# A fused linear attention and gated MLP on one core: moving tiles 256 instead of 320 bytes behind the weights

## The chip, the cores and the metric

The kernel runs on one core of a Trainium2 chip. The metric is the device time of one execution in microseconds, as the median of several runs. Instructions run on TensorE (PE in the profile, with weight loads apart as PEld), VectorE (DVE), ScalarE (ACT), GpSimd (POOL) and the DMA queues that SyncE (SP) and GpSimd issue.

## The reference

All data are float32. The reference is, cut to what is computed:

```python
# q, k, v: (8, 8, 576, 64) = batch, heads, sequence, head size
q_s = softmax of q over the head size (1e-9 added to the sum)
k_s = softmax of k over the sequence  (1e-9 added to the sum)
kv  = einsum('bhsd,bhse->bhde', k_s, v)
att = einsum('bhsd,bhde->bhse', q_s, kv)
x   = att, heads side by side: 4608 tokens x 512
out = (sigmoid(x @ w_gate) * (x @ w_val)) @ w_out    # 512 -> 1536 -> 512
```

## The kernel before

The 4608 tokens are worked through in nine windows of 512. Window 0 runs in plain fp32 while the weights are still being loaded and prepared (`g1_0`, L617, for the first product of the MLP, `g2_0`, L644, for the second, `x_mm_0`, L566, for the attention). Its weights arrive as 64-bit words that VectorE and ScalarE put together into fp32. In windows 1 to 8 each fp32 number is split into a high and a low part of type fp32r, and each product is three matmuls: high by high, high by low, low by high.

A window w of 1 to 8 takes six steps, one for each pair of blocks of 128 hidden columns. In a step:

- `g1(w, p)` (matmuls at L662) computes gate and value with a Strassen-like scheme of seven block products `prod`, 12 matmuls each, 84 in all. Weights are `a_w` (three of the products) and `s_sb` (four), the moving operand is `c_hl`, 256 columns at a time.
- `h_split` splits the result into `h`, and `g2` of the step before (L730) computes 24 matmuls of 512 columns into four accumulators: weights `h`, moving operand `wo_hl`.
- beside it stand parts of the next window's attention: key softmax, the key-value product `k_mm` (L382, plain fp32, weights in `ring`), the query softmax and `x_mm` (L542, weights `kv_sb`, moving operand in `ring`). `x_mm` cuts a window's 512 columns in two where a batch of 576 tokens ends.

The order of the instructions is written out by hand (`tc.manual_schedule()`), engine by engine in the order of the code. `s_sb` is loaded again for each step by four transfers on GpSimd's queue (L282), `wo_hl` by two (L238).

The tiles lie in pools, one behind the other in each partition, in the order in which the pools are opened: const, bpad, bpool, cpool, apad, apool, two, wpad, wpool, four, ring, small. `bpad`, `apad` and `wpad` hold one unused tile each, whose width sets where the pools behind it begin. Weights lie in const (`s_sb`, `kv_sb`, `f_last`), apool (`a_w`, `f_w`) and two (`h`); moving operands in bpool and cpool (`c_hl`, `x_0`), wpool (`wo_hl`, `wo_t`) and ring. In a partition, 128 columns of weights are 512 bytes and 256 moving columns 1024, so the places in a tile at which the matmuls of L662 and L730 start lie alike modulo 512.

In the function below, what bears on the change are the pads and the matmuls named above.

Of the kernel before, what the change touches and what calls it, by code (L numbers as in the profile page):

```python
# [8 lines left out]
F32 = mybir.dt.float32  # L9
# [8 lines left out]
P = 128  # L18
# [34 lines left out]
def attn_moe(ctx: ExitStack, tc: tile.TileContext, qf, qn, qT, k, kT, v, wg, wv, wo, out):  # L53
# [5 lines left out]
    bpad = ctx.enter_context(tc.tile_pool(name="bpad", bufs=1))  # L59
    bpool = ctx.enter_context(tc.tile_pool(name="bpool", bufs=1))  # L60
    cpool = ctx.enter_context(tc.tile_pool(name="cpool", bufs=1))
    apad = ctx.enter_context(tc.tile_pool(name="apad", bufs=1))
    apool = ctx.enter_context(tc.tile_pool(name="apool", bufs=1))
    two = ctx.enter_context(tc.tile_pool(name="two", bufs=2))
    wpad = ctx.enter_context(tc.tile_pool(name="wpad", bufs=1))
# [1 line left out]
    four = ctx.enter_context(tc.tile_pool(name="four", bufs=4))  # L67
    ring = ctx.enter_context(tc.tile_pool(name="ring", bufs=11))
    small = ctx.enter_context(tc.tile_pool(name="small", bufs=2))
    bpad.tile([P, 128], F32, name="pad_b")  # L70
    apad.tile([P, 48], F32, name="pad_a")
    wpad.tile([P, 80], F32, name="pad_w")
    dpool = ctx.enter_context(tc.tile_pool(name="dpool", bufs=2, space=bass.MemoryType.DRAM))
    spool = ctx.enter_context(tc.tile_pool(name="spool", bufs=1, space=bass.MemoryType.DRAM))
    ps_acc = ctx.enter_context(tc.tile_pool(name="ps_acc", bufs=NT, space=bass.MemoryType.PSUM))
# [1050 lines left out]
```

## Time and profile before

| | |
|---|---|
| median of 3 runs | 974.13 us (973.41 to 974.25) |
| profiled execution | 974.62 us |
| its span, first to last instruction | 972.9 us |
| mean granted TensorE clock | 0.987 |
| TensorE busy | 948.6 us, 6062 matmul records |
| VectorE, ScalarE, GpSimd busy | 613.3, 488.6, 169.7 us |
| DMA | 257.79 MB, 265 GB/s on the mean |

The span is the time between the first and the last instruction; the execution's own time has what lies around it as well. A TensorE busy share counts overlapping matmuls once and says nothing on how densely they follow one another; for that the chain of work in order of time is read, where a run of matmuls of one line is one piece with its length and count. A plain fp32 matmul leaves two records, an fp32r matmul one.

### The profile page before, as it was taken

The numbers are of one execution on the slowest core, as the hardware profiler recorded it, in microseconds if no ns is written. First come the engines' busy times: TensorE is split into PE (matmuls) and PEld (weight loads), VectorE is DVE, ScalarE is ACT, GpSimd is POOL, SyncE is SP. The second block draws the span as 40 slices with busy tenths as digits, with TensorE's granted clock in tenths as the row PEclk, the third lists the DMA queues.
The fourth block names the chain that finished last, engine by engine and source line by source line (L and its number), as shares of the span: only waits on it lengthen the run. The fifth ranks groups of instructions, "written<-read, shape, count | busy, mean of one in ns | idle before, by whom it ended". The sixth has DMA issues, their size and how long they took to land.

```text
span 972.9 us, 15630 instructions
## 1 busy us (share of the span) xinstructions
PE 948.6 (98%) x6062; PEld 821.0 (84%) x6062; DVE 613.3 (63%) x1013; ACT 488.6 (50%) x824; POOL 169.7 (17%) x316
## 2 busy tenths in 40 slices
PE   5899999899999999999999999999999999999998
PEld 4544544699999999999999999999999999999997
DVE  7698878776567566755675667556754655564242
ACT  4589785563446354725372547354635333533222
POOL 0110001221122112211211212111212121212210
PEclk8899999899999999999999999999999999999999
DMA  9987485899699978999899979997998689858672
GB/s 320 353 243 264 181 292 169 304 357 326 203 246 360 300 249 202 381 288 280 187 378 301 270 166 381 318 271 157 381 302 258 203 249 311 240 173 257 200 209 70
DMA packets 93865, 257.79 MB, mean 265 GB/s; under 512 B 15264, under 2 KB 17568, under 8 KB 93024
## 3 DMA queue, kind: packets, MB, share of 16 engines
q0 software_dynamic: 43712, 168.32, 57.6%
q1 hardware_dynamic: 50080, 88.48, 31.5%
q8 instruction: 48, 0.79, 0.4%
q14 instruction: 25, 0.20, 0.1%
HBM read 228.20 MB, written 28.56 MB: 264 GB/s over the span
## 4 chain that ended last, share of the span: by engine, by line
PE 82%; DMA 6%; issue 5%; DVE 4%; ACT 2%; POOL 0%; SPq 0%; POOLq 0%; ACTq 0%; DVEq 0%
PE gv L662 48%; PE acc L730 27%; PE at L382 3%; PE gv L542 2%; DMA lent<-v_in 1%; DMA wo_raw<-wo_in 1%; PE acc L644 1%; DMA lent<-kT_in 1%; DMA ring<-qf_in 1%; DMA s<-s_sb 1%; PE at L542 1%; DMA lent<-k_in 1%; DVE s L250 1%; DVE s_sb L273 0%; DVE a_w L273 0%
## 5 line engine op out<-in xcount | busy, mean ns | idle before, releaser
L662 PE MATMUL gv<-c_hl,s_sb 128*128 128x256 f32 x2304 | 283.7, 278 | 0.0
L662 PEld LDWEIGHTS gv<-c_hl,s_sb 128*128 128x128 f32 x2304 | 275.0, 188 | 0.0
L730 PE MATMUL acc<-wo_hl,h 128*128 128x512 f32 x1152 | 272.3, 392 | 0.0
L730 PEld LDWEIGHTS acc<-wo_hl,h 128*128 128x128 f32 x1152 | 213.0, 188 | 44.5
L662 PE MATMUL gv<-c_hl,a_w 128*128 128x256 f32 x1728 | 225.5, 279 | 0.0
L662 PEld LDWEIGHTS gv<-c_hl,a_w 128*128 128x128 f32 x1728 | 214.5, 188 | 4.3 <-issue 1.0
L282 POOL DMA_DIRECT2D s_sb<-s x188 | 100.4, 534 | 312.5 <-PE gv L662 312.4
L688 DVE TENSOR_TENSOR sg<-gv,sg 128x512 f32<-128x512 f32 x48 | 33.2, 691 | 162.0 <-PE gv L662 161.8
L238 POOL DMA_DIRECT2D wo_hl<-wo x96 | 52.6, 549 | 296.0 <-PE acc L730 295.7
L680 ACT COPY sg<-gv 128x512 f32<-128x512 f32 x48 | 28.2, 588 | 120.4 <-PE gv L662 118.7
L690 ACT COPY sg<-gv 128x512 f32<-128x512 f32 x48 | 28.2, 587 | 105.9 <-PE gv L662 105.9
L617 PE MATMUL gv<-x,f_w 128*128 128x512 f32 x160 | 72.4, 606 | 3.5 <-ACT h L625 3.5
L692 DVE TENSOR_TENSOR sg<-sg 128x512 f32<-128x512 f32 x48 | 33.2, 692 | 60.0 <-ACT sg L690 60.0
L617 PEld LDWEIGHTS gv<-x,f_w 128*128 128x128 f32 x160 | 30.5, 194 | 41.7 <-issue 35.8
L713 DVE TENSOR_TENSOR h<-sg,h 128x1024 fp32r<-128x1024 f32 x48 | 58.8, 1226 | 1.6
L701 DVE TENSOR_TENSOR sg<-sg 128x512 f32<-128x512 f32 x48 | 33.3, 693 | 33.5 <-ACT sg L695 33.5
L695 ACT ACTIVATE sg<-sg 128x512 f32<-128x512 f32 x48 | 30.4, 633 | 47.7 <-DVE sg L694 47.7
L644 PE MATMUL acc<-wo_t,h 128*128 128x512 f32 x96 | 46.0, 625 | 5.6 <-DVE h L629 5.6
L685 ACT COPY sg<-gv 128x512 f32<-128x512 f32 x48 | 28.2, 587 | 38.8 <-PE gv L662 38.8
L682 ACT COPY sg<-gv 128x512 f32<-128x512 f32 x48 | 28.2, 587 | 38.4 <-PE gv L662 38.4
L644 PEld LDWEIGHTS acc<-wo_t,h 128*128 128x128 f32 x96 | 19.2, 202 | 30.1 <-issue 22.2
L694 DVE TENSOR_TENSOR sg<-gv,sg 128x512 f32<-128x512 f32 x48 | 33.2, 692 | 4.1
(152 smaller groups left out, 1040.5 us busy)
## 6 DMA issues: line engine op xcount, KB each, us to landing
s_sb<-s POOLq DMA_DIRECT2D x188, 512.0 KB, 7.4
wo_hl<-wo POOLq DMA_DIRECT2D x96, 512.0 KB, 6.3
s<-s_sb POOLq DMA_DIRECT2D x6, 2048.0 KB, 7.6
out<-x SPq DMA_DIRECT2D x36, 256.0 KB, 10.0
ring<-k_in SPq DMA_DIRECT2D x28, 256.0 KB, 13.8
ring<-qn_in SPq DMA_DIRECT2D x28, 256.0 KB, 9.9
q_b<-q_m_row SPq DMA_DIRECT2D x56, 128.0 KB, 8.9
ring<-qT_in SPq DMA_DIRECT2D x28, 256.0 KB, 8.7
```

The source lines that it names most:

```text
L238: nc.gpsimd.dma_start(out=t.rearrange("p h e -> p (h e)"), in_=wo_dram[2 * p + i].bitcast(F32R))
L282: nc.gpsimd.dma_start(out=s_sb[:, i].rearrange("p h n e -> p (h n e)"), in_=s_dram[p][:, i * n:(i + 1) * n].bitcast(F32R),)
L617: nc.tensor.matmul(ps[n], lhsT=w[:, kt // 2, sl], rhs=x_0[:, kt], start=(kt == 0), stop=(kt == NK - 1),)
L644: nc.tensor.matmul(acc[0][m], lhsT=h_0[j][:, m * P:(m + 1) * P], rhs=wo_t[j // 2][:, j % 2], start=(j == 0), stop=(j == NJ - 1),)
L662: nc.tensor.matmul(ps[:, n], lhsT=lh(kt), rhs=c_hl[i][:, x, kt], start=(first and n == 0 and kt == 0 and lh is wh and x == 0), stop=(last ...
L688: nc.vector.tensor_tensor(out=sg[:, 0], in0=rr, in1=sg[:, 0], op=ALU.add)
L692: nc.vector.tensor_tensor(out=sg[:, 3], in0=sg[:, 3], in1=sg[:, 2], op=ALU.add)
L694: nc.vector.tensor_tensor(out=sg[:, 1], in0=z, in1=sg[:, 1], op=ALU.add)
L695: nc.scalar.activation(sg[:, 0:2, 0], sg[:, 0:2, 0], AF.Sigmoid)
L701: tt(out=sg[:, 0:2, 0], in0=sg[:, 0:2, 0], in1=sg[:, 0:2, 1], op=ALU.mult)
L713: nc.vector.tensor_tensor(out=lo, in0=sg[:, :, 0], in1=hi.bitcast(F32), op=ALU.subtract)
L730: nc.tensor.matmul(acc[w][m], lhsT=h[lh][:, i, sl], rhs=o[i][:, rh], start=(at == 0 and i == 0 and lh == 0 and rh == 0), stop=(at == NS - ...
```

## The change

Three unused tiles get another width: 448, 256 and 256 bytes in place of 512, 192 and 320.

```diff
-    bpad.tile([P, 128], F32, name="pad_b")
-    apad.tile([P, 48], F32, name="pad_a")
-    wpad.tile([P, 80], F32, name="pad_w")
+    bpad.tile([P, 112], F32, name="pad_b")
+    apad.tile([P, 64], F32, name="pad_a")
+    wpad.tile([P, 64], F32, name="pad_w")
```

In the built program every engine has the same instructions in the same order before and after. What differs are start addresses: the pools bpool, cpool, wpool, four, ring and small begin 64 bytes lower, the others where they were. Start addresses in a partition, modulo 512:

| pool | holds | before | after |
|---|---|---|---|
| const | `s_sb`, `kv_sb`, `f_last` (weights) | 128 | 128 |
| apool | `a_w`, `f_w` (weights) | 128 | 128 |
| two | `h` (weights), `q_0` | 128 | 128 |
| bpool, cpool | `c_hl`, `x_0` (moving) | 448 | 384 |
| wpool | `wo_hl`, `wo_t` (moving) | 448 | 384 |
| ring | queries (moving), keys (weights of L382) | 448 | 384 |

## Prediction

> **What bounds the kernel now.** I read the engine table first, then the chain of work that ended last, then who waited for whom.
>
> ```profile
> span 972.9 us, 15630 instructions
> ...
> PE 948.6 (98%) x6062; PEld 821.0 (84%) x6062; DVE 613.3 (63%) x1013; ACT 488.6 (50%) x824; POOL 169.7 (17%) x316
> ...
> PEclk8899999899999999999999999999999999999999
> ...
> PE 82%; DMA 6%; issue 5%; DVE 4%; ACT 2%; POOL 0%; SPq 0%; POOLq 0%; ACTq 0%; DVEq 0%
> PE gv L662 48%; PE acc L730 27%; PE at L382 3%; PE gv L542 2%; DMA lent<-v_in 1%; DMA wo_raw<-wo_in 1%; PE acc L644 1%; DMA lent<-kT_in 1%; DMA ring<-qf_in 1%; DMA s<-s_sb 1%; PE at L542 1%; DMA lent<-k_in 1%; DVE s L250 1%; DVE s_sb L273 0%; DVE a_w L273 0%
> ```
>
> TensorE is busy for 98% of the span, at a full granted clock in nearly every slice. Two lines carry three quarters of the chain: L662, the first MLP product, and L730, the second. So the time is their matmul count times the distance from one matmul to the next. The waits on TensorE say whether anything else comes in between.
>
> ```profile
> engine line waited for: us in total, times, longest us
> PE acc L369 <- ACT lent L361: 7.9, 2, 4.3
> PE acc L644 <- DVE h L629: 5.6, 1, 5.6
> PE gv L617 <- ACT h L625: 3.5, 1, 3.5
> PE acc L942 <- DVE lent L939: 1.8, 1, 1.8
> ```
>
> Every line here belongs to window 0 and what leads up to it, which ends at 181 us. From there to the tail TensorE waits for no other engine and no transfer long enough to be listed, so its own pace is the whole story. The chain in order of time gives that pace: its columns are start, length and piece, and one piece of L662 with x84 is one full pass over a pair of weight blocks.
>
> ```profile
> 209.57 9.52 PE gv L662 x84
> 229.46 9.89 PE gv L662 x84
> ...
> 309.90 9.89 PE gv L662 x84
> 330.17 9.52 PE gv L662 x84
> 345.18 9.52 PE gv L662 x84
> ...
> 408.32 9.52 PE gv L662 x84
> 428.20 9.89 PE gv L662 x84
> ...
> 561.39 9.92 PE gv L662 x84
> 576.81 9.52 PE gv L662 x84
> ...
> 948.27 9.89 PE gv L662 x84
> ```
>
> There are 48 such blocks, and they have two lengths: 15 take 9.52 us (113.3 ns a matmul) and 33 take 9.89 to 9.97 us (117.7 ns), with nothing in between. The 84 instructions are the same each time, on the same engine at the same clock, and all their moving tiles begin 320 bytes behind the weights. So this offset alone does not set the pace: one and the same offset gives both. What differs is the state in which a block is entered; the level holds through many blocks in a row and flips where other matmuls or a short wait came between (330 us, 428 us, 576 us).
>
> The blocks of L730 between them, 24 matmuls each, show the same thing fainter:
>
> ```profile
> 239.35 5.51 PE acc L730 x24
> ...
> 339.69 5.49 PE acc L730 x24
> ```
>
> 5.49 us is 228.8 ns a matmul, for twice the columns of L662. All in all L662 is 15 x 9.52 + 33 x 9.89 = 469.2 us and L730 48 x 5.5 = 264 us: together 733 us, the 75% of the chain.
>
> **The change, part by part.** No instruction is added, removed or moved, on any engine or queue. Only addresses change: bpool, cpool, wpool, four, ring and small lie 64 bytes lower, the others stay. By the addresses of the built program the moving tiles of L662, L730, L617 and L644 go from 320 to 256 bytes behind their weights (modulo 512); L542 goes from 320 to 256 and, in the second piece of the odd windows, from 64 to 0; L382 from 192 to 256. The question is what 64 bytes do to the distance between matmuls. The trace holds two places where offsets differ for like work.
>
> The first is L542, the product of queries and key-values, cut in two where a batch ends. In window 3 the pieces are 192 and 320 columns wide, in window 5 320 and 192. The first piece begins at 320, the second 768 or 1280 bytes on, which is 64 modulo 512. So the wide piece lies at 64 in one window and at 320 in the other:
>
> ```profile
> 360.20 2.31 PE gv L542 x18
> 362.51 0.77 PE at L542 x6
> ...
> 558.33 2.29 PE gv L542 x18
> 560.62 0.77 PE at L542 x6
> ```
>
> 2.31 against 2.29 us and 0.77 against 0.77: moving the wide piece by 256 bytes shows nothing beyond 0.02 us. The second place is the plain fp32 work of window 0. L566 has weights and moving tile at the same place modulo 512 (offset 0), L644 at 320, both 128x512:
>
> ```profile
> 32.18 3.70 PE L566 MATMUL acc<-q,f_last 128*128 128x512 f32 x8
> ...
> 85.76 3.60 PE L644 MATMUL acc<-wo_t,h 128*128 128x512 f32 x8
> ...
>   PE acc L566: 0.2, 1
> ```
>
> 3.70 us holds a wait of 0.2 us (last line), 3.60 none: no price of the offset to be seen there either. Neither place is a long run of fp32r matmuls at one offset, so they bound L662 and L730 loosely.
>
> L662, 4032 matmuls, all on the path. Lower end: all blocks at the short length, 33 x (9.89 - 9.52) = -12.2 us. Upper end: the two levels lie 0.37 us a block apart; a further step of that size, 10.27 us for all 48, gives 48 x 10.27 - 469.2 = +23.8 us. I take 0: the level comes from the state at entry, and the state is dealt anew, about one block in three short as now.
>
> L730, 1152 matmuls, all on the path. The nearest rows are its own two lengths, 0.02 us apart, 48 x 0.02 = 1.0 us either way. As an outer bound goes the step of L662 (0.37 us over 84, 4.4 ns a matmul): 5.1 us either way. I take 0, for the spread within L730 itself is far nearer.
>
> L542, under 200 matmuls: the two windows differ by 0.02 us; with 4.4 ns each the bound is 0.9 us either way. Taken as 0.
>
> L382 and window 0, fp32. L382 has some 280 records on the path; 3.70 against 3.60 over 8 records, wait and all, is 12 ns a record, +3.4 us at most, and the same below as nothing excludes a gain. I take 0, for the wait explains the difference. In window 0 L617 and L644 move too, but the chain runs through other things there:
>
> ```profile
> 49.48 11.55 DMA wo_raw<-wo_in
> ...
> 149.76 7.71 DMA s<-s_sb
> 157.54 2.17 ACT s_sb L269 x4
> ```
>
> What TensorE gains or loses there is mostly covered by the loads and by VectorE and ScalarE; if the cover is gone, 12 ns on 288 records is 3.5 us.
>
> VectorE, ScalarE and the transfers write the same tiles 64 bytes lower. I take 0. They are hidden by TensorE: VectorE is busy 63%, ScalarE 50%, and they and the POOL queue wait for it.
>
> ```profile
> POOL s_sb L282 <- PE gv L662: 312.4, 185, 6.1
> POOL wo_hl L238 <- PE acc L730: 295.7, 92, 8.5
> DVE sg L688 <- PE gv L662: 161.8, 43, 7.9
> ```
>
> If TensorE became 12 us faster, a pass and its second product would be 0.37 us shorter, against single waits of up to 6 to 8 us on these engines; the cover would hold.
>
> The sum is 0 on 972.9 us of span. The profiled execution took 974.62 us, 1.7 us around the span and 0.5 us above the median of the runs, 974.13; I put the forecast at 974.5 us.
>
> **Rivals.** *Slower: the two streams meet more often.* If the next weights, which are loaded while a matmul streams, collide with the moving tile in memory, then the 117.7 ns blocks are blocks with one collision more than the 113.3 ns ones, and an offset of 256 may add a further one. The place is L662; each block that gains a step costs 0.37 us, and from 6 blocks on (2.2 us) it decides the sign. All blocks at 10.27 us give 974.6 + 23.8 = 998.4 us. For it speaks that one offset already shows two levels in whole steps, so a third is near, and that the present levels could be the lower ones of a ladder. Also, if the pattern repeats every 256 bytes, as L542 allows (64 as good as 320), then 256 is the same as no offset. Against it: the fp32 matmuls at offset 0 pay nothing.
>
> *Faster: all blocks short.* The 113.3 ns state is stable for 6 blocks in a row (330 to 408 us). If 64 bytes less take away the collision that separates the levels, 33 blocks fall to 9.52 us: 974.6 - 12.2 = 962.4 us. Against it: at 320 this state is the rarer one, and it is lost again after 408 us.
>
> *Nothing at all: the offset enters nowhere.* Then even the deal of levels stays, and the time is 974.6 us within the spread of the runs (973.41 to 974.25). For it speak both comparisons above. Against it: something makes the same block 0.37 us longer, and it isn't named. The Trainium skill, TensorE: Matmul & The Clock Gate, Step-by-step: what each phase is for, states it as a rule: the array reads memory through two independent ports, one for the moving operand and one for the weights, and loading the next tile's weights takes no read bandwidth from the running matmul. By that rule the change does nothing. The trace agrees in L542 and L566; it doesn't bear it out in L662 and L730. The same page (Back-to-back issue gap) gives N/2.4 + 2.5 ns, 215.8 ns for 512 columns where the trace has 228.8; if the change took that whole difference away, and that of 256 columns (109.2 ns), I estimate from the page 1152 x 13.0 + 15 x 84 x 4.1 + 33 x 84 x 8.5 = 44 us less.
>
> **How the numbers follow.** Levels kept, dealt anew: 0.40. Slower rival: 0.30. Faster rival: 0.18. Nothing at all: 0.12. A new deal moves whole windows of six blocks, 6 x 0.37 = 2.2 us each, so this case has a range of its own of 970 to 979 us, two windows either way. The runs of this kernel can tell about 0.2% (2 us) from no change. Of the 0.40, 0.11 are faster, 0.16 the same and 0.13 slower, a little more than faster since the fp32 work can add. With the rivals: faster 0.11 + 0.18 = 0.29, same 0.16 + 0.12 = 0.28, slower 0.13 + 0.30 = 0.43. Slower is the largest side, though the likeliest single case is no change. The range goes from 961 (all blocks short, and some L730) to 999 (all blocks one step up); I leave 0.07 below it and 0.10 above, for levels that no row of this trace shows.
>
> **What would show it.** In the chain of the changed kernel the L662 pieces with x84 should again be 9.52 or 9.89 us long, about a third of them short, the L730 pieces with x24 5.49 or 5.51 us, and the two L542 pieces 2.3 and 0.77 us. Pieces of 10.2 us or more show the slower rival, pieces of 9.52 throughout the faster one, the same lengths at the same places the third. The first L662 piece should start near 181 us. I am wrong if a new length appears in L662, or if L730, which I count at nothing, moves by more than 0.1 us a piece.

## The result, and the profile after

The changed kernel takes 986.15 us (986.00 to 986.76, 4 runs) against 973.98 us before (973.41 to 974.25, 4 runs): a ratio of 1.0124, with a 95% interval of 1.0108 to 1.014. It is 1.2% slower. The profiled execution took 986.2 us with a span of 984.4 us, 11.5 us more than the span before.

The engine table and the part of the chain by engine, from the page of the changed kernel:

```profile
PE 958.9 (97%) x6062; PEld 832.6 (85%) x6062; DVE 612.8 (62%) x1013; ACT 488.7 (50%) x824; POOL 168.4 (17%) x316
...
PE 89%; DMA 7%; DVE 2%; ACT 1%; issue 1%; POOL 0%; SPq 0%; POOLq 0%; DVEq 0%
PE gv L662 48%; PE acc L730 27%; PE gv L617 5%; PE at L382 3%; PE acc L644 3%; PE gv L542 2%; DMA s<-s_sb 2%; DMA ring<-qf_in 1%; DMA kmax_row<-k_max 1%; DMA sg<-wv_in 1%; PE at L542 1%; DMA lent<-v_in 1%; DMA s_sb<-s 1%; DMA lent<-k_in 1%; DVE s_sb L273 0%
```

VectorE, ScalarE and GpSimd have the busy times of before, within 1.3 us; TensorE alone has 10 us more. Its mean granted clock is 0.989 against 0.987 before, so a slower clock is not the reason. The chain in order of time (start, length, piece) shows where:

```profile
229.19 10.07 PE gv L662 x84
239.27 5.47 PE acc L730 x24
...
330.75 10.07 PE gv L662 x84
340.82 5.47 PE acc L730 x24
...
567.12 10.08 PE gv L662 x84
...
582.67 10.07 PE gv L662 x84
...
944.20 10.07 PE gv L662 x84
```

The two lengths of before, 9.52 and 9.89 us, are gone. Every steady block now takes 10.07 us, 120 ns a matmul, whatever came before it, and L730 takes 5.47 us in place of 5.49 and 5.51 (behind L382, 5.68 in place of 5.71 and 5.72). The groups of the page say the same about one instruction:

```profile
L662 PE MATMUL gv<-c_hl,s_sb 128*128 128x256 f32 x2304 | 292.4, 283 | 0.2 <-DMA s_sb<-s 0.2
L662 PEld LDWEIGHTS gv<-c_hl,s_sb 128*128 128x128 f32 x2304 | 283.4, 192 | 0.4 <-issue 0.4
```

The matmul's record lasts 283 ns where it lasted 278 on the mean. The weight load, which runs beside the matmul ahead of it, lasts 192 ns, not 188, though nothing about the weights has changed: both have become longer.

The sum of the difference: L662 goes from 469.2 us to 48 x 10.07 = 483.4 us, +14.2. L730, added up from start to start of its matmuls, goes from 264.4 to 262.9 us, -1.5. The first block of L662 starts 1.6 us earlier, as these two rows of the line's own view show (duration min/median/max in ns, then first and last start in us; before, then after):

```profile
L662 PE MATMUL gv<-c_hl,a_w x72: 278/279/682, 180.3 to 203.8; 128*128 128x256 f32 x72
```

```profile
L662 PE MATMUL gv<-c_hl,a_w x72: 277/283/682, 178.7 to 203.0; 128*128 128x256 f32 x72
```

That makes +11.1 us; the 0.2 us that one block waits for a load of `s_sb`, and pieces of some tenths, make up the rest of 11.5. The earlier start is no effect of the offset: in the kernels below it lies between 178.6 and 180.6 us in both directions.

### The profile page after: what moved, and what is told of

Read it like the earlier page. It is cut to its first block, busy times and chain, and to the rows that moved or that the text cites. A ratio compares the mean times of both kernels' runs of the same rounds, so it can differ in the third digit from the quotient of the medians.

```text
span 984.4 us, 15630 instructions
## 1 busy us (share of the span) xinstructions
PE 958.9 (97%) x6062; PEld 832.6 (85%) x6062; DVE 612.8 (62%) x1013; ACT 488.7 (50%) x824; POOL 168.4 (17%) x316
## 4 chain that ended last, share of the span: by engine, by line
PE 89%; DMA 7%; DVE 2%; ACT 1%; issue 1%; POOL 0%; SPq 0%; POOLq 0%; DVEq 0%
PE gv L662 48%; PE acc L730 27%; PE gv L617 5%; PE at L382 3%; PE acc L644 3%; PE gv L542 2%; DMA s<-s_sb 2%; DMA ring<-qf_in 1%; DMA kmax_row<-k_max 1%; DMA sg<-wv_in 1%; PE at L542 1%; DMA lent<-v_in 1%; DMA s_sb<-s 1%; DMA lent<-k_in 1%; DVE s_sb L273 0%
## 5 line engine op out<-in xcount | busy, mean ns | idle before, releaser
L662 PE MATMUL gv<-c_hl,s_sb 128*128 128x256 f32 x2304 | 292.4, 283 | 0.2 <-DMA s_sb<-s 0.2
L662 PEld LDWEIGHTS gv<-c_hl,s_sb 128*128 128x128 f32 x2304 | 283.4, 192 | 0.4 <-issue 0.4
L730 PE MATMUL acc<-wo_hl,h 128*128 128x512 f32 x1152 | 270.8, 391 | 0.0
L730 PEld LDWEIGHTS acc<-wo_hl,h 128*128 128x128 f32 x1152 | 213.2, 188 | 43.2
L662 PE MATMUL gv<-c_hl,a_w 128*128 128x256 f32 x1728 | 231.4, 283 | 0.0
L662 PEld LDWEIGHTS gv<-c_hl,a_w 128*128 128x128 f32 x1728 | 220.2, 192 | 4.3 <-issue 0.7
L617 PE MATMUL gv<-x,f_w 128*128 128x512 f32 x160 | 72.3, 605 | 3.4 <-ACT h L625 3.4
L617 PEld LDWEIGHTS gv<-x,f_w 128*128 128x128 f32 x160 | 30.5, 194 | 41.5 <-issue 35.8
```

The source lines that it names most:

```text
L617: nc.tensor.matmul(ps[n], lhsT=w[:, kt // 2, sl], rhs=x_0[:, kt], start=(kt == 0), stop=(kt == NK - 1),)
L662: nc.tensor.matmul(ps[:, n], lhsT=lh(kt), rhs=c_hl[i][:, x, kt], start=(first and n == 0 and kt == 0 and lh is wh and x == 0), stop=(last ...
L730: nc.tensor.matmul(acc[w][m], lhsT=h[lh][:, i, sl], rhs=o[i][:, rh], start=(at == 0 and i == 0 and lh == 0 and rh == 0), stop=(at == NS - ...
```

## The experiments

All kernels differ from the kernel before in pads alone. Line numbers are those of before. Each profile is of one execution, so the counts of blocks below are of one execution per kernel. The theory after the result: a matmul streams its moving tile while the next weights are loaded, and what the two cost each other depends on the distance of their addresses (*pairs*). The rivals: the moved tiles are slow for their absolute place, or because other engines and transfers write them there (*places*, *traffic*).

### c_hl alone, wo_hl alone

`g1_256`, `c_hl` and `x_0` at 256 behind the weights, all else at 320:

```diff
-    bpad.tile([P, 128], F32, name="pad_b")
-    apad.tile([P, 48], F32, name="pad_a")
+    bpad.tile([P, 112], F32, name="pad_b")
+    apad.tile([P, 64], F32, name="pad_a")
```

> Only bpool and cpool move: c_hl and x_0 lie 256 bytes behind their weights, wo_hl, wo_t and the ring stay at 320. Theory of pairs (the pace of a line follows from the place of its own moving tile against its own weights): L662 pieces of 84 all 10.07 us as after the change, L730 pieces 5.49 to 5.51 us as before; time 974 + 14 = 988 us. Theory of traffic (other engines and transfers that write the moved wpool, four and ring tiles slow TensorE): L662 pieces 9.52 and 9.89 us, time 974 us.

Measured: 993.22 us against 975.06, ratio 1.0183 (1.0146 to 1.022). Its chain:

```profile
333.00 10.07 PE gv L662 x84
343.08 5.60 PE acc L730 x24
348.68 10.08 PE gv L662 x84
```

L662 is slow throughout with `c_hl` moved alone, so traffic into wpool, four and the ring isn't needed for it. The time was missed by 5 us: L730, whose tiles lie as before, takes 5.60 us after a slow L662, not 5.49. By the starts of the matmuls within a block, 41 of its 48 blocks run at 233.3 to 233.5 ns a matmul, the six behind L382 at 234.0 and the first at 229.7; before, all but the six behind L382 run at 228.7 to 229.4. So the pace of a line depends on more than its own offset; what differs here is the line ahead of it.

`g2_256`, `wo_hl`, `wo_t` and the ring at 256, `c_hl` at 320:

```diff
-    wpad.tile([P, 80], F32, name="pad_w")
+    wpad.tile([P, 64], F32, name="pad_w")
```

> Only wpool, four, ring and small move: wo_hl, wo_t and the ring lie at 256, c_hl and x_0 stay at 320. Theory of pairs: L730 pieces 5.47 us, L662 pieces 9.52 or 9.89 us with a deal of their own; time 972.5 us if the deal stays 15 to 33, 961 to 978 us at its ends. Theory of traffic: L662 pieces 10.07 us, time 986 us.

Measured: 979.02 us, ratio 1.0037 (1.0018 to 1.0056). The kernel before ran between 972.16 and 979.48 us on that chip, more widely than on the first, so a few tenths of a per cent are read from the profile.

```profile
329.21 9.89 PE gv L662 x84
339.10 5.48 PE acc L730 x24
344.58 9.89 PE gv L662 x84
354.48 5.48 PE acc L730 x24
```

L730 has nearly the length of after. L662 has only its own two lengths of before, but 47 blocks of 48 are long where 33 were; the 44 that an expectation below gives is too low. That is +5.3 us of L662 for -1.2 us of L730.

### Place or distance

`shift_all`: weights and moving tiles all 64 bytes lower modulo 512, the distance still 320.

```diff
-    bpad = ctx.enter_context(tc.tile_pool(name="bpad", bufs=1))
...
-    bpad.tile([P, 128], F32, name="pad_b")
...
-    s_sb = const.tile([P, 4, 2, 2, 2 * P], F32R, name="s_sb")
+    const.tile([P, 112], F32, name="pad_c"); s_sb = const.tile([P, 4, 2, 2, 2 * P], F32R, name="s_sb")
```

> 448 bytes of padding at the front of const and none in bpad: every tile, weights and moving, lies 64 bytes lower modulo 512 than before, moving tiles at 384 as after the change, but still 320 behind the weights. Theory of pairs: all as before, L662 9.52 and 9.89, L730 5.49 to 5.51, time 974 us (970 to 979 with another deal). Theory of absolute places (a moving tile at 384 is slow whatever the weights): L662 pieces 10.07 us, time 986 us.

Measured: 974.55 us, ratio 0.9995 (0.9976 to 1.0014).

```profile
406.46 9.52 PE gv L662 x84
415.99 4.66 PE at L382 x40
420.64 5.71 PE acc L730 x24
426.35 9.89 PE gv L662 x84
```

Both lengths of before are back, 16 short and 32 long, with the moving tiles where the change put them modulo 512. The flip shown, behind the key-value product of L382, stands in the step where it stood before; in the first two windows the deal differs.

`weights_up`: the reverse. The moving tiles stay at 448 as before; 64 bytes in front of const raise the weights to 192.

```diff
-    bpad.tile([P, 128], F32, name="pad_b")
-    apad.tile([P, 48], F32, name="pad_a")
-    wpad.tile([P, 80], F32, name="pad_w")
+    bpad.tile([P, 112], F32, name="pad_b")
+    apad.tile([P, 64], F32, name="pad_a")
+    wpad.tile([P, 64], F32, name="pad_w")
...
-    s_sb = const.tile([P, 4, 2, 2, 2 * P], F32R, name="s_sb")
+    const.tile([P, 16], F32, name="pad_c"); s_sb = const.tile([P, 4, 2, 2, 2 * P], F32R, name="s_sb")
```

> The moving tiles stay at 448 modulo 512 as before the change; the weights move up 64 bytes, from 128 to 192, so the moving tiles lie 256 behind them. Theory of pairs: as after the change, L662 10.07 us throughout with weight loads of 192 ns, L730 5.47 us, time 986 us. Theory that the place or the writing of the moved tiles counts: as before, L662 9.52 and 9.89 us, time 974 us.

Measured: 986.43 us, ratio 1.0115 (1.0086 to 1.0144), the result of the change.

```profile
230.46 10.07 PE gv L662 x84
240.53 5.47 PE acc L730 x24
```

```profile
L662 PEld LDWEIGHTS gv<-c_hl,s_sb x2304: 192/192/192, 182.2 to 969.2; 128*128 128x128 f32 x192
```

The long weight loads are back as well. The moving tiles at 448 are slow here and were not before; at 384 they are slow after the change and not in `shift_all`. So neither their place nor who writes them there counts; the distance between moving tile and weights does.

### Which distances

The diffs from here on show the three pads as they are in the kernel, in place of 128, 48 and 80.

`off_64`:

```diff
+    bpad.tile([P, 64], F32, name="pad_b")
+    apad.tile([P, 112], F32, name="pad_a")
+    wpad.tile([P, 16], F32, name="pad_w")
```

> All moving tiles 64 bytes behind the weights. If the pattern repeats every 256 bytes (as L542 seemed to allow), 64 is the same as 320: L662 9.52 and 9.89 us, L730 5.49 to 5.51, time 974 us. If it repeats every 512 bytes only, other lengths come out; L662 between 9.5 and 10.1 us and a time of 960 to 990 us. If the distance to the same place counts (the nearer the worse), 64 is worse than 256: over 10.07 us, over 986 us.

It took 974.42 us, ratio 0.9999 (0.9968 to 1.0029):

```profile
409.17 9.52 PE gv L662 x84
418.70 4.66 PE at L382 x40
423.35 5.71 PE acc L730 x24
429.06 9.89 PE gv L662 x84
```

It is the kernel before again, down to the deal: 15 blocks short, 33 long, the flips behind the same steps. 64 and 320 are one and the same, so the pattern seems to repeat every 256 bytes, and 256 should be as good as no distance; no kernel here has L662 at 0 itself.

`off_128`:

```diff
+    bpad.tile([P, 80], F32, name="pad_b")
+    apad.tile([P, 96], F32, name="pad_a")
+    wpad.tile([P, 32], F32, name="pad_w")
```

> All moving tiles 128 bytes behind the weights. 320 and 64 gave the same lengths, so the pattern repeats after 256 bytes or a part of it that 64 isn't. If it repeats every 128 bytes, 128 is the same as 256: L662 10.07 us, L730 5.47 us, time 986 us. If every 256 bytes, 128 is a third kind: if the distance to the same place counts it is the farthest of all and L662 is 9.52 us throughout, time about 962 us; if not, another length.

One run of 987.09 us. L662 lengths are 9.96 and 9.97 us, with some of 10.08, L730 5.58 and 5.60:

```profile
228.74 9.96 PE gv L662 x84
238.70 5.60 PE acc L730 x24
244.30 9.97 PE gv L662 x84
254.27 5.58 PE acc L730 x24
```

128 is a third kind, its lengths unlike those at 256, so the pattern doesn't repeat every 128 bytes, and the farthest distance is not the best.

`off_192`:

```diff
+    bpad.tile([P, 96], F32, name="pad_b")
+    apad.tile([P, 80], F32, name="pad_a")
+    wpad.tile([P, 48], F32, name="pad_w")
```

> All moving tiles 192 bytes behind the weights. Repeating every 128 bytes: the same as 64 and 320, L662 9.52 and 9.89 us, L730 5.49 to 5.51 us, time 974 us. Repeating every 256 bytes: a fourth kind, between 128 and 256 in its lengths, time 962 to 986 us.

One run of 972.75 us. L662 has 30 short blocks against 15 before, and L730 pays for it with 5.59 us a block:

```profile
777.44 9.53 PE gv L662 x84
786.96 5.59 PE acc L730 x24
792.56 9.53 PE gv L662 x84
```

Over all, L662 takes 5.1 us less than before and L730 4.5 us more, by the starts of the matmuls.

`off_32`:

```diff
+    bpad.tile([P, 56], F32, name="pad_b")
+    apad.tile([P, 120], F32, name="pad_a")
+    wpad.tile([P, 8], F32, name="pad_w")
```

> All moving tiles 32 bytes behind the weights, half a step between 256 (as 0) and 320 (as 64). If the memory is read in pieces of 64 bytes, 32 is either as 0 (L662 10.07 us, 986 us) or as 64 (9.52 and 9.89 us, 974 us), or worse than both since every piece is split. If in smaller pieces, L662 lies between, 9.5 to 10.07 us, 974 to 986 us.

One run of 980.67 us. One length only, 9.80 us, and L730 at its longest:

```profile
229.83 9.80 PE gv L662 x84
239.63 5.60 PE acc L730 x24
```

So steps under 64 bytes count too.

### Putting the better distances together

Since 192 had most short blocks in L662 and 256 the shortest L730, they were put together, and each with 320.

`g1_192_g2_256`:

```diff
+    bpad.tile([P, 96], F32, name="pad_b")
+    apad.tile([P, 80], F32, name="pad_a")
+    wpad.tile([P, 64], F32, name="pad_w")
```

> c_hl and x_0 192 bytes behind the weights, wo_hl and the ring 256: the better place of each line as measured so far. Theory of pairs alone (each line by its own offset): L730 5.47 us, L662 9.52 us for 30 blocks or more, 17 or fewer at 9.89; time 972.7 - 48 x 0.13 = 966.5 us or less, 960 if all blocks are short. If the state in which L730 at 256 leaves TensorE decides (with c_hl at 320 it left 44 of 48 blocks long): L662 9.89 us nearly throughout, time 973 us.

Measured 976.81 us, ratio 1.0025 (1.0011 to 1.0039). The second rival was right: L730 is at its shortest ever, 5.44 us, and leaves L662 in the long state. By the starts of the matmuls L662 takes 5.6 us more than before and L730 2.6 us less, which is the measured +3.0 us; the 973 us expected for this case left out the first.

```profile
778.57 9.89 PE gv L662 x84
788.46 5.44 PE acc L730 x24
793.90 9.89 PE gv L662 x84
```

`g1_192_g2_320`:

```diff
+    bpad.tile([P, 96], F32, name="pad_b")
+    apad.tile([P, 80], F32, name="pad_a")
+    wpad.tile([P, 80], F32, name="pad_w")
```

> c_hl and x_0 at 192, wo_hl and the ring at 320 as before the change. Pairs alone: L730 5.49 us, L662 at least 30 short blocks of 9.52 us; time 967.5 us, 961 if all are short. If the state that L730 leaves decides: the deal of before, 15 short and 33 long, 974 us, or another.

Measured 977.79 us, ratio 1.0031 (1.0009 to 1.0053).

```profile
778.40 9.89 PE gv L662 x84
788.28 5.51 PE acc L730 x24
793.80 9.89 PE gv L662 x84
```

`c_hl` lies as in `off_192`, at the same point of the same window; only what L730 and the ring have is changed, and 30 short blocks have become 6. Five of the six stand right behind L542; of the 39 that stand right behind L730 none is short, where 25 were in `off_192`. So the two lengths are one offset's two states, and the lines ahead choose.

`g1_224_g2_256`:

```diff
+    bpad.tile([P, 104], F32, name="pad_b")
+    apad.tile([P, 72], F32, name="pad_a")
+    wpad.tile([P, 64], F32, name="pad_w")
```

> c_hl and x_0 at 224, between 192 (9.52 and 9.89 us) and 256 (10.07 us), wo_hl at 256. At 32, between 0 and 64, L662 was 9.80 us throughout. If the two sides of 0 are alike, 224 gives about 9.80 us too and 972 us; if the pace falls steadily away from 0, 9.7 to 9.9 us; if one side is clear of the collision, 9.52 us throughout and 960 us.

One run of 980.78 us: one length of 9.94 us, L730 5.46. The two sides of 256 are not alike (9.80 at 32, 9.94 at 224), and the pace does not fall clear.

`g1_96_g2_256`:

```diff
+    bpad.tile([P, 72], F32, name="pad_b")
+    apad.tile([P, 104], F32, name="pad_a")
+    wpad.tile([P, 64], F32, name="pad_w")
```

> c_hl and x_0 at 96, wo_hl and the ring at 256. So far a matmul of L662 takes 120.0 ns at 0, 116.7 at 32, 113.3 or 117.8 at 64, 118.6 at 128. If the line from 0 over 32 to 64 goes on, 110 ns at 96, L662 9.24 us, L730 5.47 us, time about 944 us. If 96 lies between 64 and 128, L662 9.5 to 9.96 us and 960 to 978 us. If nothing under 113.3 ns is to be had because the weight loads themselves then set the pace, L662 is 9.52 us at best and the time 960 us.

Measured 987.60 us, ratio 1.0129 (1.0107 to 1.0152).

```profile
229.16 10.08 PE gv L662 x84
239.24 5.49 PE acc L730 x24
244.72 10.08 PE gv L662 x84
```

The line from 0 over 32 to 64 does not go on; 96 is as slow as 256. The weight loads are not longer there, though:

```profile
L662 PEld LDWEIGHTS gv<-c_hl,s_sb 128*128 128x128 f32 x2304 | 283.0, 188 | 0.0
```

So a load of 192 ns goes with the slow pace at 256 bytes, but isn't what every slow pace has.

All steady lengths of an L662 block in us, by the distance of `c_hl` modulo 256 (0 stands for 256, and 96 and 224 were run with `wo_hl` at 256 alone):

| 0 | 32 | 64 | 96 | 128 | 192 | 224 |
|---|---|---|---|---|---|---|
| 10.07 | 9.80 | 9.52 or 9.89 | 10.08 | 9.96 to 10.08 | 9.52 or 9.89 | 9.94 |

No kernel of these is shown to beat the one before: `off_192` has one run, 972.75 us, 0.2 us under the fastest of the 7 runs of before beside it (972.96 to 976.98 us) and within the spread of the 15 that came next on that chip (971.87 to 978.91 us).

## Why the prediction was right or wrong

**The forecast case did not come.** 986.15 us lies within 961 to 999 and on the side with the largest chance, slower with 0.43. But the likeliest case, levels kept and dealt anew at 974.5 us, did not come: the levels were replaced by a single third one. The case that came is the rival named slower, with a chance of 0.30. That range and side held is owed to the room left for this rival; the sum itself, 974.5 us, was 11.7 us too low, so the hit does not speak for it.

**What bounds the kernel** was read rightly. The distance from one matmul to the next in L662 and L730 makes +12.7 us, the start that came 1.6 us earlier takes that much off again, and no wait of note was added.

**The step that failed is "L662 ... I take 0".** It measured +14.2 us. It rested on L542, whose wide piece lies at 64 in one window and at 320 in the other with nothing between them. `off_64` shows why that told nothing: at 64 and at 320 L662 has the same lengths, so the two windows compared equal distances. The row was right, and as evidence it was empty; the prediction had said in the rival's sentence that L542 allows such a pattern, and that 256 would then be as good as no offset, and still counted L542 against any effect. In fact L542 does react, in both directions. In window 4, where both pieces have 256 columns and lie at 64 before and at 0 after (modulo 256), the first 18 matmuls get longer (first row before, second after); from start to start a matmul goes from 117.9 to 119.7 ns, and in `off_32` it takes 116.7. These are nearly the paces of L662 at the same distances. In window 8 its 512 columns go from 229.2 to 226.7 ns, as L730 does. All 180 matmuls of the line together take 27.7 us before and 27.6 after, so the total hides both.

```profile
459.00 2.12 PE gv L542 x18
```

```profile
463.05 2.15 PE gv L542 x18
```

L566 was the second support. It is plain fp32, and plain fp32 indeed does not care: L617 takes the same with `x_0` at 256 (second row, after) as at 320 (first row, before), while L662 pays 0.2 to 0.6 us a block; and in all 14 kernels, at seven distances modulo 256, L617 takes 93.7 to 93.9 us from start to start:

```profile
89.20 7.03 PE L617 MATMUL gv<-x,f_w 128*128 128x512 f32 x16
```

```profile
77.36 7.03 PE L617 MATMUL gv<-x,f_w 128*128 128x512 f32 x16
```

So neither place could price the fp32r lines.

**The slower rival: right place and sign, price too high, mechanism open in part.** It put a further step of 0.37 us on top, 10.27 us a block and 998.4 us; the third level lies at 10.07 us, 0.18 us above the second. Its sum of +23.8 us measured +14.2. What it says of the mechanism, a collision between weight load and moving stream, agrees with the weight loads of 192 ns at this distance and with `shift_all` and `weights_up`, which show that the distance between the two counts. The collision itself isn't shown: 96 bytes are as slow without longer weight loads, and L730 gets faster at the distance at which L662 gets slower. That more collisions in whole steps make the levels isn't shown either, and lengths of 9.80, 9.94 and 9.97 us speak against a ladder.

**The deal by the state at entry** fits what was seen at 320, 64 and 192 bytes (`g2_256`, `g1_192_g2_320`). It failed for 256, where 48 blocks have one length: whether there is a second state depends on the distance itself, so the offset sets the pace after all, which the prediction had put down to the state alone.

**L730** was counted at 0 with 1.0 us either way by its own rows, 5.1 at most: it measured -1.5 us, more than its own rows gave. **L542**, taken as 0, was right in sum: 2.30 and 0.78 us in window 5 after the change, with the second piece at 0, where it took 2.29 and 0.77 before.

```profile
564.04 2.30 PE gv L542 x18
566.34 0.78 PE at L542 x6
```

**Window 0 and L382** at 0 were right within the 2.0 us by which the start of L662 varies between kernels (178.6 to 180.6 us).

**Nothing at all**, the rival that the Trainium skill states as a rule (TensorE: Matmul & The Clock Gate, Step-by-step: what each phase is for: two independent read ports, so loading the next weights takes nothing from the running matmul), fell. With the weights moved 64 bytes and the moving tiles left in place (`weights_up`), the same matmuls go from 9.52 and 9.89 to 10.07 us. For the plain fp32 matmuls of this kernel no run speaks against the rule; for its fp32r ones the distance between the two operands sets the pace, which by the rule it should not.

**What stays open**: whether and where the two streams meet in the memory, why 96 is as slow as 0 and 192 as fast as 64, why 512 columns are fastest at the distance at which 256 are slow, and what the state is that one line hands to the next. No run separates these.

## What to carry to other kernels

Where TensorE runs without waits, read the length of equal blocks of matmuls in the chain of work: two lengths for the same instructions mean that something beside the instructions sets the pace, and pads that only move addresses can cost over 1% (1.2% for this change, 1.8% in `g1_256`). Before two rows are used to show that an offset does not matter, see that they differ in what might matter: distances 256 bytes apart gave the same lengths here. See also that a sum does not hide two effects of opposite sign, as in L542. And tune such pads for all lines together, since a line at its best distance can leave the next one in its worse state.

## What the runs showed of the hardware that was not expected

- The pace of fp32r matmuls with 256 columns depends on where the moving tile starts relative to the weights, with 64 and 320 bytes alike: 113.3 to 120.0 ns a matmul, 6%, with nothing but addresses changed. For 512 columns in L730, behind a block of L662, it is 226.7 to 233.5 ns, and the distance of 256 bytes, among the slowest for 256 columns, is the fastest there.
- At 64 (or 320) and 192 bytes the same stream of L662 has two stable paces, 113.3 and 117.8 ns, kept for whole blocks and handed on through other matmuls.
- The weight load of L662 itself gets longer, 192 against 188 ns, at the distance of 256 bytes, but not at 96, where the matmuls are as slow.
- Plain fp32 matmuls show none of it: 16 records of L617 take 7.03 us at 320 and at 256, and the line's total is 93.7 to 93.9 us in all 14 kernels.
